# Dealing w3's rows to the partitions in neighbouring pairs, in a strided sparse attention and feed-forward kernel

## The chip, the cores and the metric

The kernel runs on one core of one Trainium2 chip. The metric is the device time of one execution in microseconds (us), and the median over several runs is compared. The engines are named as in the profile: PE is TensorE's matmul row and PEld its weight loads, DVE is VectorE, ACT is ScalarE, POOL is GpSimd, SP is SyncE. DMA transfers are issued from the queues of POOL and SP and run on 16 shared DMA engines.

## What is computed

Eight batches of 8 heads, 576 tokens and a head size of 64 go through attention. Heads 0 to 3 see a local window of 32 positions, heads 4 to 7 see every 32nd position. The result is laid out as 4,608 tokens by 512 and goes through a feed-forward part:

```python
scores = scale * np.matmul(q, k.transpose(0, 1, 3, 2))
scores = np.where(masks[None, :, :, :], scores, -1000000000.0)
scores = scores - np.max(scores, axis=-1, keepdims=True)
attn = np.exp(scores)
attn = attn / (np.sum(attn, axis=-1, keepdims=True) + 1e-09)
attn_out = np.matmul(attn, v)
...
a = x @ w1                 # 4608 x 512 by 512 x 1024
b = x @ w2
h = a * b @ w3             # 1024 x 1024
out = h @ w_out            # 1024 x 512
```

All inputs and the output are fp32; the kernel computes in fp16 with fp32 sums.

## The kernel before

**Weights.** Since nothing stands between `w3` and `w_out`, the kernel multiplies them once into `wfh` (1,024 rows by 512), and the feed-forward part becomes `(a * b) @ wfh`. All weight loads are issued from POOL and turn fp32 into fp16 on the way. `load_w3` (L210) brings two blocks of 128 rows of w3 at a time into a tile `w3s` of 128 partitions by 2 by 1,024; by the view `w3r` (L199), partition p gets rows 128 c + p and 128 (c + 1) + p, so a partition's data are two separate rows of 4 KB in memory. `load_wo` (L207) brings w_out in two halves; by the view `wor` (L200) partition p holds rows 8 p to 8 p + 7, so a half is four neighbouring rows, 8 KB in one piece. `load_w` (L203) brings w1 and w2, each in two halves of 512 columns.

**Folding.** For each of the eight blocks mc of w3's rows, `fold_t(mc)` (L218) transposes the block on PE with eight matmuls against the identity. The block is the stationary operand and is read with a step of 8 columns (L223). The result goes through PSUM into a tile `w3T` (L225). `fold_m(mc, half)` (L228) multiplies it with `woh`, four matmuls a half (L233), and after the second half the sum is copied into `wfh[:, mc, :]` (L236). Partition p of `wfh[:, mc, :]` thus belongs to the row of w3 that partition p of block mc holds.

**Feed-forward pieces.** Tokens are taken in nine chunks of 512. `emit_a(c, jc)` (L238) computes 128 columns of `x @ w1` for a chunk with four matmuls of 512 columns (L243); the weights are the stationary operand, `w1h[:, ci, jc * P:(jc + 1) * P]`. ACT copies the sum to SBUF (L247). `emit_b(c, jc)` (L250) does the same with w2 (L253), and DVE multiplies both into `abt[:, jc, :]` (L256). `emit_out` (L258) multiplies `abt` with `wfh` over all eight jc (L264), copies and stores 128 tokens. Row p of `abt[:, jc, :]` must be the same feed-forward column as partition p of `wfh[:, jc, :]`.

**Attention.** For each batch there are four pairs of heads, 32 units in all. `load_qk` (L88) and `load_v` (L108) load a unit, the q and k loads and the strided v loads from POOL, the local v loads from SP. `emit_T` transposes q and k on PE (L296), `emit_S` makes the scores (L328 local, L334 strided), `emit_max`, `emit_sub`, `emit_exp` and `emit_norm` do the softmax on DVE, ACT and POOL, `emit_P` transposes the probabilities (L396, or by DMA from unit 9 on, L391), and `emit_V` multiplies with v (L416, L433) and writes the transposed `x` into `xT`.

**Order.** Everything is issued in an order written out by hand (L498 to L714). Each engine and each DMA queue works in its own order of issue. In the start-up (L499 to L618) the first units of attention, the weight loads and the folding are interleaved: POOL issues four q and k loads of units 0 and 1, then k of unit 2, `load_w3(2, 2)`, the masks, q of unit 2, `load_w3(4, 2)`, `load_wo(0)`, unit 3, `load_wo(4)`, and later `load_w3(6, 2)` and `load_w3(0, 2)`, then w1 and w2. PE transposes units 0 and 1, makes the scores of unit 0, then comes `fold_t(2)`, the scores of unit 1, the transposes of unit 2, `fold_t(3)`, `fold_t(4)`, `fold_t(5)`, the scores of unit 2, and `fold_m(5, 0)`, the first that needs w_out. From L619 on, `feed(us, batches)` (L470) puts feed-forward pieces between the attention units: `next_piece` (L452) picks the next `emit_a`, `emit_b` or `emit_out` and counts 0.87 us for a piece of the first two kinds and twice that for the last. This order depends on counts alone, not on which columns a piece covers.

Of the kernel before, what the change touches and what calls it, by code (L numbers as in the profile page):

```python
# [9 lines left out]
FP16 = mybir.dt.float16  # L10
# [17 lines left out]
def kernel(  # L28
# [11 lines left out]
    nc = tc.nc  # L40
    B, H, S, D = q.shape
    DM = H * D
    DF = moe_w3.shape[0]
    NTOK = B * S
    P = 128
# [16 lines left out]
    wst = ctx.enter_context(tc.tile_pool(name="wst", bufs=2))  # L62
# [117 lines left out]
    w1h = wpool.tile([P, KC1, DF], FP16, name="w1h")  # L180
    w2h = wpool.tile([P, KC1, DF], FP16, name="w2h")
# [14 lines left out]

    w1r = moe_w1.rearrange("(c p) n -> p c n", p=P)
    w2r = moe_w2.rearrange("(c p) n -> p c n", p=P)
    w3r = moe_w3.rearrange("(c p) n -> p c n", p=P)  # L199
    wor = moe_w_out.rearrange("(p c) n -> p c n", p=P)  # L200
    w3st = {}

# [4 lines left out]
    def load_wo(c):  # L207
        nc.gpsimd.dma_start(woh[:, c:c + 4, :], wor[:, c:c + 4, :])

    def load_w3(c, n=1):  # L210
        w3 = wst.tile([P, n, DF], FP16, tag="w3s%d" % n, bufs=4 if n > 1 else 2, name="w3s")
        nc.gpsimd.dma_start(w3, w3r[:, c:c + n, :])
        for i in range(n):
            w3st[c + i] = w3[:, i, :]

# [12 lines left out]
    def fold_m(mc, half, eng=nc.scalar.copy):  # L228
# [6 lines left out]
        if half:  # L235
            eng(out=wfh[:, mc, :], in_=ps)  # L236

    def emit_a(c, jc):  # L238
        if jc == 0:
            abts[c] = ffn.tile([P, KC2, NT], FP16, tag="abt", name="abt")  # L240
        aps = psF.tile([P, NT], FP32, tag="f", name="aps")
        for ci in range(KC1):
            nc.tensor.matmul(aps, w1h[:, ci, jc * P:(jc + 1) * P],  # L243
                             xT[ci][:, c * NT:(c + 1) * NT], start=(ci == 0),
                             stop=(ci == KC1 - 1))
        asb = ffn.tile([P, NT], FP32, tag="asb", name="asb")
        nc.scalar.copy(out=asb, in_=aps)  # L247
        abts[c, jc] = asb

    def emit_b(c, jc):  # L250
        bps = psF.tile([P, NT], FP32, tag="f", name="bps")
        for ci in range(KC1):
            nc.tensor.matmul(bps, w2h[:, ci, jc * P:(jc + 1) * P],  # L253
                             xT[ci][:, c * NT:(c + 1) * NT], start=(ci == 0),
                             stop=(ci == KC1 - 1))
        nc.vector.tensor_mul(abts[c][:, jc, :], bps, abts.pop((c, jc)))  # L256
# [195 lines left out]
    def next_piece(batches):  # L452

        a, o = state["ab"], state["out"]
        c, j = divmod(a, 2 * KC2)
        can_ab = c < NCH and NT * c + NT <= S * batches and c < o // (NT // P) + 2
        oc, ot = divmod(o, NT // P)
        can_out = oc < NCH and a >= 2 * KC2 * (oc + 1) + (0 if c >= NCH else 2)
        late = not can_ab and oc < NCH and a >= 2 * KC2 * (oc + 1)
        if (can_out and (state["turn"] >= 4 or not can_ab)) or late:  # L460
            state["out"] += 1
            state["turn"] = 0
            return 2 * T_A, lambda: emit_out(oc, ot)
        if can_ab:
            state["ab"] += 1
            state["turn"] += 1
            return T_A, lambda: (emit_a, emit_b)[j % 2](c, j // 2)
        return None
# [29 lines left out]
    with tc.manual_schedule():  # L498
# [7 lines left out]
        load_qk(2, "k")  # L506
        emit_cast_v(1, cp)
        load_w3(2, 2)
        make_identity(nc, id16)
        make_maskL()  # L510
        zero_L(0)
        load_qk(2, "q")
        emit_T(0)
        load_w3(4, 2)
        emit_T(1)
        make_sel()
# [22 lines left out]
        emit_exp(1)  # L539
        emit_norm(0, dve)  # L540
        load_w3(6, 2)
        load_qk(4, "k")
        fold_m(4, 0)
# [202 lines left out]
```

## Time and profile before

| | |
|---|---|
| median of three runs | 269.75 us |
| the three runs | 269.6, 269.75, 272.18 us |
| the profiled execution: time | 272.12 us |
| the profiled execution: span from the first to the last instruction | 270.4 us |
| TensorE clock granted | 1.000 |
| four w3 loads, 512 KB each as fp16 | issue 794 ns in the mean, 7.5 us median from issue to landing |
| two w_out loads, 512 KB each as fp16 | issue 682 ns in the mean, 9.8 us to landing |
| 288 matmuls of w1, 288 of w2 | 74.0 and 73.9 us of PE's busy time |
| weight loads of w1 and w2 | 98 ns in the mean |

One execution was recorded by the hardware profiler. The page gives the busy time of each engine, the span in 40 equal slices of 6.8 us with a digit for the tenths in which an engine was busy, the DMA queues, the chain of work that ended last (followed back from the last instruction to whatever released each step), and the costliest groups of instructions. The trace behind it holds each instruction and each DMA packet with start and duration, so stretches of the span, the timeline of one engine and the waits of a tile can be asked for. A busy PE is not PE at its peak: matmuls overlap, so the pace is read from the distance between starts.

### The profile page before, as it was taken

The numbers are of one execution on the slowest core, as the hardware profiler recorded it, in microseconds if no ns is written. First come the engines' busy times: TensorE is split into PE (matmuls) and PEld (weight loads), VectorE is DVE, ScalarE is ACT, GpSimd is POOL, SyncE is SP. The second block draws the span as 40 slices with busy tenths as digits, with TensorE's granted clock in tenths as the row PEclk, the third lists the DMA queues.
The fourth block names the chain that finished last, engine by engine and source line by source line (L and its number), as shares of the span: only waits on it lengthen the run. The fifth ranks groups of instructions, "written<-read, shape, count | busy, mean of one in ns | idle before, by whom it ended". The sixth has DMA issues, their size and how long they took to land.

```text
span 270.4 us, 9826 instructions
## 1 busy us (share of the span) xinstructions
PE 252.0 (93%) x4186; PEld 131.5 (49%) x4186; DVE 176.2 (65%) x353; ACT 140.9 (52%) x256; POOL 153.0 (57%) x236
## 2 busy tenths in 40 slices
PE   0488999999999999899999999999999999999995
PEld 0374566445554454455555455544554444444443
DVE  2468998777788867867886788678767823332210
ACT  1561678565755654656466555545655534333322
POOL 8847767398975895489558965887674110000000
PEclk9999999999999999999999999999999999999999
DMA  7999997999999999999989998998465152001113
GB/s 118 184 199 196 190 196 113 209 164 207 221 207 156 114 229 147 172 124 211 166 129 180 221 173 77 238 189 107 85 174 102 30 93 94 2 0 71 47 55 142
DMA packets 66749, 38.75 MB, mean 143 GB/s; under 512 B 45588, under 2 KB 60944, under 8 KB 66704
## 3 DMA queue, kind: packets, MB, share of 16 engines
q0 software_dynamic: 22624, 17.29, 43.6%
q1 hardware_dynamic: 44080, 20.82, 38.2%
q8 instruction: 33, 0.54, 0.8%
q14 instruction: 12, 0.10, 0.1%
HBM read 39.24 MB, written 9.44 MB: 180 GB/s over the span
## 4 chain that ended last, share of the span: by engine, by line
PE 75%; DMA 8%; DVE 8%; POOL 4%; ACT 2%; issue 2%; SPq 0%; DVEq 0%; POOLq 0%; ACTq 0%
PE ops L264 22%; PE aps L243 19%; PE bps L253 19%; PE fps L233 4%; DMA woh<-in_moe_w_out_dram 3%; DMA pT<-prL 3%; PE op L416 2%; PE tpq L296 2%; POOL s L105 2%; PE sp L328 2%; DMA vhS<-in_v_dram 2%; DVE mx L348 1%; PE op L433 1%; PE sp L334 1%; DVE tmp L340 1%
## 5 line engine op out<-in xcount | busy, mean ns | idle before, releaser
L243 PE MATMUL aps<-xT,w1h 128*128 128x512 f16 x288 | 74.0, 379 | 0.1
L253 PE MATMUL bps<-xT,w2h 128*128 128x512 f16 x288 | 73.9, 379 | 0.0
L256 DVE TENSOR_TENSOR abt<-bps,asb 128x512 f16<-128x512 f32 x72 | 47.7, 678 | 32.7 <-PE bps L253 29.7
L264 PE MATMUL ops<-wfh,abt 128*128 128x512 f16 (+1 forms) x296 | 65.6, 374 | 0.0
L247 ACT COPY asb<-aps 128x512 f32<-128x512 f32 x72 | 41.4, 585 | 33.1 <-PE aps L243 20.1
L130 POOL DMA_DIRECT2D vhS<-in_v_dram x70 | 42.5, 717 | 5.5 <-DMA woh<-in_moe_w_out_dram 2.3
L253 PEld LDWEIGHTS <-w2h 128*128 128x128 f16 x288 | 28.2, 98 | 34.0
L264 PEld LDWEIGHTS <-abt 128*128 128x128 f16 x296 | 27.8, 98 | 30.4
L243 PEld LDWEIGHTS <-w1h 128*128 128x128 f16 x288 | 27.0, 98 | 30.7
L378 POOL TENSOR_TENSOR prS<-prS,rc 128x594 f16<-128x594 f16 x14 | 17.0, 1217 | 38.5 <-ACT asb L247 16.0
L269 ACT COPY osb<-ops 128x512 f32<-128x512 f32 (+1 forms) x36 | 20.8, 578 | 29.6 <-PE ops L264 26.7
L355 DVE TENSOR_TENSOR tmp<-tmp,mx 128x576 f32<-128x576 f32 (+1 forms) x32 | 26.1, 816 | 0.9
L105 POOL DMA_DIRECT2D s<-in_q_dram x35 | 21.0, 637 | 8.5 <-PE aps L243 3.3
L348 DVE TENSOR_REDUCE mx<-tmp 128x9 f32<-128x576 f32 (+1 forms) x32 | 24.2, 757 | 0.5
L296 PE MATMUL tpq<-id,s 54*64 54x54 f16 (+1 forms) x640 | 17.5, 196 | 7.5 <-DMA s<-in_q_dram 6.8
L105 POOL DMA_DIRECT2D s<-in_k_dram x35 | 21.4, 665 | 1.5 <-DMA s<-in_q_dram 0.9
L378 POOL TENSOR_TENSOR prL<-prL,rc 128x576 f16<-128x576 f16 x15 | 18.0, 1203 | 5.5 <-ACT osb L269 3.9
L367 ACT ACTIVATE prS<-tmp 128x594 f16<-128x594 f32 x16 | 11.2, 702 | 18.7 <-DVE tmp L355 13.1
L296 PEld LDWEIGHTS <-s 54*64 54x64 f16 (+1 forms) x1280 | 14.5, 111 | 11.5 <-DMA s<-in_q_dram 6.8
L375 DVE TENSOR_REDUCE sm<-prL 128x9 f32<-128x576 f16 x16 | 12.0, 749 | 11.3 <-ACT prL L367 11.3
L375 DVE TENSOR_REDUCE sm<-prS 128x11 f32<-128x594 f16 x16 | 12.3, 770 | 10.6 <-ACT prS L367 10.6
L296 PE MATMUL tpk<-id,s 54*64 54x54 f16 (+1 forms) x640 | 17.3, 196 | 2.0 <-DMA s<-in_k_dram 1.7
(78 smaller groups left out, 273.5 us busy)
## 6 DMA issues: line engine op xcount, KB each, us to landing
out_dram<-osb SPq DMA_DIRECT2D x35, 256.0 KB, 3.6
vsL<-in_v_dram SPq DMA_DIRECT2D x32, 128.0 KB, 5.3
s<-in_q_dram POOLq DMA_DIRECT2D x16, 144.0 KB, 4.8
s<-in_k_dram POOLq DMA_DIRECT2D x16, 144.0 KB, 4.9
s<-in_k_dram POOLq DMA_DIRECT2D x31, 74.2 KB, 4.9
s<-in_q_dram POOLq DMA_DIRECT2D x31, 74.2 KB, 4.8
w3s<-in_moe_w_dram POOLq DMA_DIRECT2D x4, 512.0 KB, 7.5
vhL<-vhL SPq DMA_DIRECT2D x16, 120.0 KB, 4.3
```

What stands on the lines that cost most here:

```text
L105: nc.gpsimd.dma_start(t[p0 + r0[0]:p0 + r0[1], h, 0:n * D], _ap(src[b, h0 + h], 0 + ap[0], ap[1] + [[1, n * D]]))
L130: nc.gpsimd.dma_start(vt[HALF * half + r0[0]:HALF * half + r0[1], h, 0:m * D], _ap(v[b, h0 + h], 6 * half * D + ap[0], ap[1] + [[1, m * D]]))
L243: nc.tensor.matmul(aps, w1h[:, ci, jc * P:(jc + 1) * P], xT[ci][:, c * NT:(c + 1) * NT], start=(ci == 0), stop=(ci == KC1 - 1))
L247: nc.scalar.copy(out=asb, in_=aps)
L253: nc.tensor.matmul(bps, w2h[:, ci, jc * P:(jc + 1) * P], xT[ci][:, c * NT:(c + 1) * NT], start=(ci == 0), stop=(ci == KC1 - 1))
L256: nc.vector.tensor_mul(abts[c][:, jc, :], bps, abts.pop((c, jc)))
L264: nc.tensor.matmul(ps, abts[c][:, jc, ts * P:(ts + 1) * P], wfh[:, jc, n * w:n * w + w], start=(jc == 0), stop=(jc == KC2 - 1))
L296: nc.tensor.transpose(tp[HALF * h:HALF * h + HALF, s, :], s16[p0:p0 + npar, h, s * D:(s + 1) * D], id16[p0:p0 + npar, p0:p0 + npar])
L348: nc.vector.tensor_reduce(out=mx, in_=tmp, axis=AX.X, op=ALU.max)
L355: nc.vector.tensor_tensor(out=tmp, in0=tmp, in1=_sub(mx, 0, P, 0, [[1, nt], [0, w]]), op=ALU.subtract)
L375: nc.vector.tensor_reduce(out=sm, in_=prv, axis=AX.X, op=ALU.add)
L378: eng.tensor_tensor(out=prv, in0=prv, in1=_sub(rc, 0, P, 0, [[1, nt], [0, w]]), op=ALU.mult)
```

## The change

The view `w3r` gives partition p the rows 256 u + 2 p and 256 u + 2 p + 1 of pair u: two neighbouring rows, 8 KB in one piece. `load_w3` copies them as one run of 2,048 columns per partition into the same tile. Block mc of w3 then holds, in partition p, row 256 (mc // 2) + 2 p + mc % 2. To match, `emit_a` and `emit_b` take for piece jc the columns 256 (jc // 2) + jc % 2 + 2 p of w1 and w2: every second column. `fold_t`, `fold_m`, `emit_out`, the order of issue and the sizes of all tiles are as before.

```diff
-    w3r = moe_w3.rearrange("(c p) n -> p c n", p=P)
+    w3r = moe_w3.rearrange("(c p i) n -> p c (i n)", p=P, i=2)
...
-    def load_w3(c, n=1):
-        w3 = wst.tile([P, n, DF], FP16, tag="w3s%d" % n, bufs=4 if n > 1 else 2, name="w3s")
-        nc.gpsimd.dma_start(w3, w3r[:, c:c + n, :])
+    def load_w3(c, n=2):
+        w3 = wst.tile([P, n, DF], FP16, tag="w3s", bufs=4, name="w3s")
+        nc.gpsimd.dma_start(w3.rearrange("p i n -> p (i n)"), w3r[:, c // 2, :])
         for i in range(n):
             w3st[c + i] = w3[:, i, :]
...
+    def cols(jc):
+        n0 = 2 * P * (jc // 2) + jc % 2
+        return slice(n0, n0 + 2 * P - 1, 2)
+
     def emit_a(c, jc):
...
-            nc.tensor.matmul(aps, w1h[:, ci, jc * P:(jc + 1) * P],
+            nc.tensor.matmul(aps, w1h[:, ci, cols(jc)],
                              xT[ci][:, c * NT:(c + 1) * NT], start=(ci == 0),
                              stop=(ci == KC1 - 1))
...
     def emit_b(c, jc):
...
-            nc.tensor.matmul(bps, w2h[:, ci, jc * P:(jc + 1) * P],
+            nc.tensor.matmul(bps, w2h[:, ci, cols(jc)],
                              xT[ci][:, c * NT:(c + 1) * NT], start=(ci == 0),
                              stop=(ci == KC1 - 1))
```

## The prediction

> **What bounds the kernel now.** I read the page's busy table and slices first, then the chain of work that ended last in order of time, then the stretches of the start-up, then the rows of the two tiles that the diff touches.
>
> ```profile
> span 270.4 us, 9826 instructions
> PE 252.0 (93%) x4186; PEld 131.5 (49%) x4186; DVE 176.2 (65%) x353; ACT 140.9 (52%) x256; POOL 153.0 (57%) x236
> ...
> PE   0488999999999999899999999999999999999995
> ...
> DMA  7999997999999999999989998998465152001113
> ```
>
> PE is full from the fifth slice nearly to the end, and the DMA engines are full from the second. So after the start-up only PE time counts: in the matmul records after 47 us the start-to-start gaps above 130 ns beyond the usual pace sum to 3.4 us, the longest 1.1 us. Before 47 us it is the chain that counts:
>
> ```profile
> 5.14 0.75 POOL w3s L212
> ...
> 8.88 0.74 POOL w3s L212
> ...
> 10.63 9.24 DMA woh<-in_moe_w_out_dram
> ...
> 19.92 5.20 PE fps L233 x16
> ...
> 47.03 0.97 PE aps L243 x4
> ```
>
> The columns are start, length, engine and tile. The first half of w_out is issued at 10.63 and lands 9.24 us later, and PE's folding starts on it. Two of the four w3 loads (issued at 5.0 and 8.8) stand ahead of it on the same queue. PE's timeline shows what else waits for them:
>
> ```profile
> 13.21 1.08 PE L223 MATMUL w3tp<-id,w3s 128*128 128x128 f16 x8 [1.08 <-DMA w3s<-in_moe_w_dram]
> ...
> 17.11 1.93 PE L223 MATMUL w3tp<-id,w3s 128*128 128x128 f16 x16 [0.49 <-DMA w3s<-in_moe_w_dram]
> ...
> 19.92 5.20 PE L233 MATMUL fps<-woh,w3T 128*128 128x512 f16 x16 [0.43 <-DMA woh<-in_moe_w_out_dram]
> ```
>
> In brackets is PE's idle time and what ended it. All three waits end with a transfer that the change speeds up or that queues behind one.
>
> **Part 1, the w3 loads.** Four loads of 512 KB go from 256 packets to 128 packets each. A packet's size in the trace is that of the fp16 written, half of the fp32 read: 2,048 B becomes 4,096 B. The new shape is already in the kernel: w_out loads four neighbouring rows of 512 columns per partition, 4,096 B written. In the packet records the median packet of w3 takes 173 ns and that of w_out 324 ns, so two old packets cost 346 ns and a new one 324: 22 ns saved, times 128 packets over 16 engines = 0.18 us a load, 0.35 us for the two ahead of w_out. By the means (199 and 193 against 358 and 327 ns) a load would save 8 x (392 - 342) = 0.4 us, 0.8 us for two. But packet times overlap on an engine, and the stretches show the pace that comes out (start and end; then busy time by engine; the last two columns are DMA share and GB/s):
>
> ```profile
> 8.50:10.00 1.50, 0.69 (x34) 0.56 (x35) 0.00 (x0) 0.75 (x3) 1.43 (x4) 1.00 1.03 185
> 12.50:14.00 1.50, 0.79 (x8) 0.80 (x8) 1.43 (x4) 0.06 (x1) 1.50 (x3) 1.00 1.09 194
> 15.00:16.50 1.50, 1.50 (x52) 1.30 (x44) 1.50 (x5) 1.15 (x3) 1.00 (x2) 1.00 1.07 209
> 24.00:26.00 2.00, 1.58 (x50) 0.72 (x47) 0.81 (x3) 0.32 (x1) 1.00 (x2) 1.00 1.14 207
> ```
>
> The first two are the early w3 loads, at about 190 GB/s; the third is mostly w_out, at 209; the fourth is the third w3 load with the short packets, at 207. So when the engines are full, short packets move as many bytes as long ones, and the gain is at most the early shortfall: 524 KB at 190 GB/s is 2.76 us, at 209 it is 2.51, so 0.25 us a load and 0.5 us for two; at least it is 0. I take the middle, 0.25 us earlier for w_out, since the early stretch is the right place but the later w3 load shows that length alone does not make the difference. The bounds are 0 and 0.5.
>
> The Trainium skill, "DMA: Bandwidth & Descriptors", section Anatomy of one DMA, prices a load as a fixed 2.0 us plus its bytes over 436 GB/s, with no term for packet length at these sizes; by it this part is worth 0, and the 207 against 209 agrees, the 190 does not.
>
> POOL's issue: a w3 issue takes 794 ns in the mean, the w_out issue in the new shape 682, so about 0.1 us less for each of four. POOL is on the chain up to 10.63, but the DMA engines are already full by then (share 1.03 to 1.09), so w_out's landing is set by the queue and I cost it at 0. If that cover were gone it would be another 0.2 us of gain. POOL's two later waits on w3s (1.3 and 1.7 us) end a little earlier; they hold up q, k and v loads that are used later, so 0.
>
> What 0.25 us earlier on w_out is worth at the end: PE's work, DVE's (which idles 1.16 us at 25.6 for PE and then 0.33 us at 31.6 for the w3 transposes) and POOL's norm at 40.9 follow from the 19.92 start, so I pass it on whole. What is late next is the second pair's transposes and the scores before 19.49, but they wait for the second w3 load, which moves too. PE's first matmuls there run at 427 ns each and at 216 from 23.2 us on; if that change of pace keeps its time, 0.25 us of slow matmuls is worth half, 0.13 us. Bounds of part 1 at the end: 0 to 0.5 us of gain, I take 0.25.
>
> **Part 2, the strided weights.** Each of the 576 weight loads of w1 and w2 now reads every second column. A matmul and its weight load are two records on two rows, and only the slower one shows:
>
> ```profile
> L223 PEld LDWEIGHTS <-w3s x64: 142/149/169, 13.2 to 37.7; 128*128 128x128 f16 x64
> ...
> L243 PEld LDWEIGHTS <-w1h x288: 95/98/99, 47.0 to 258.7; 128*128 128x128 f16 x144
> ```
>
> These are minimum, median and maximum in ns. L223 is the one load in this kernel with a step, of 8 columns: 143 ns at the fast clock against 98 packed, 45 ns more. Step 2 lies between. The 512-column matmul starts every 216 ns, and 143 is still under that, so 562 of the 576 loads stay hidden under the matmul before; the cover would be gone only above 216 ns. The other 14 follow small attention matmuls (from L296, L334 and L416), and in 13 of them the records show 111 to 125 ns from the last small matmul to the first of w1 (281 ns in the other): there the load is exposed. 14 x 45 ns = 0.63 us is the upper bound, 0 the lower, as no row gives a reason for a load with a step to be shorter than a packed one. Step 2 is nearest to the packed row, one sixth of the way in step, so I take 6 ns, 0.1 us.
>
> The Trainium skill, "SBUF — State Buffer", section Specifications (TRN2), says that reads want at least two hits per 16-byte line; every second fp16 still hits a line four times, so by it this part is 0. The 143 ns at a step of 16 bytes, one hit a line, agrees; no run here shows a step of 4 bytes.
>
> **What costs nothing.** The order of the work is the same. Pieces jc 0 to 3 still read only columns 0 to 511, so each waits for the same half of w1 and w2 as before. The transposes of w3 keep their step of 8, the fold and output matmuls their shapes; only the rows they carry are permuted.
>
> **Sum.** -0.25 + 0.1 = -0.15 us. The profiled execution took 272.12 us (span 270.4 and 1.7 around it), so it would give 272.0. It lies 2.4 us above the median of the runs, 269.75, and beside the highest, 272.18; the same change on the median gives 269.6.
>
> **Rivals.**
> *The packets change nothing* (the change does not do what it says): the 207 against 209 GB/s speaks for it, the 190 against. Then 0 + 0.1: 269.85 us. The byte price of the Trainium skill's DMA page would give this too.
> *Strided loads slow every step*: the step-8 transposes start 60 ns apart at the fast clock, the packed ones of L396 56, so 4.4 ns more per pair of load and matmul. If that is added to each pair instead of hidden, 576 x 4.4 ns = 2.5 us, and 0.6 for the exposed loads: 272.9 us, slower. At the slow clock the step-8 ones are 107 ns apart, with nothing added, which speaks for a load that is just the longer of two, and against this rival. It decides once a pair costs over 4.7 ns more (2.7 us).
> *PE's fast clock comes at another time*: 3.3 us of matmuls at 427 ns stand at 19.92, eight of them, 1.69 us more than at 216. If the earlier start meets the fast clock at once, 268.0 us; if one more such stretch follows, 271.3. The Trainium skill, "TensorE: Matmul & The Clock Gate", Part 1, says that the window that decides this runs free at 3.4 us, so both are possible; the trace's 3.3 us agrees.
> *The runs' spread*: one of three runs is 2.4 us above the other two, so a median may fall there, at 272.0.
>
> **How the numbers follow.** Forecast, between -0.5 and +0.6 us (269.2 to 270.4): 0.58. Packets nothing: 0.13. Strided loads: 0.09. Clock earlier 0.05, later 0.06. Spread: 0.09. The predicted time is 269.6 us. The range reaches from 268.8, which leaves out the clock's earlier case and a few hundredths of combinations, to 272.3, which leaves out the strided rival: about 0.15 outside. A measurement of this kernel can tell about 1% from no change, 2.7 us. Faster by more needs two gains together, 0.04; slower by more is the strided rival and the spread with a loss on top, 0.10; within 1%: 0.86.
>
> **What would show it.** Right: w3s packets of 4,096 B at 205 GB/s or more before 14 us, w_out landing before 19.9, the first w1 matmul before 47.0, L243 and L253 weight loads of 98 to 143 ns, matmul steps of 216 ns. Wrong: a w1 or w2 step above 218 ns; a first w1 matmul later than 47.2; w_out landing no earlier with faster w3 loads; a new wait on PE after 47 us.

## The result and the profile after

| | before | changed |
|---|---|---|
| median of six runs each | 270.18 us | 279.78 us |
| lowest and highest | 269.57 and 272.85 | 277.24 and 283.74 |
| profiled execution: time, span | 272.12, 270.4 | 277.24, 275.5 |

The ratio is 1.0308, with a 95% interval from 1.0262 to 1.0354; it leaves out the run of 283.74 us, which fell in a slower state. The change made the kernel 3% slower, 8.3 us by the ratio and 9.6 us between the medians, where 269.6 us and a range up to 272.3 had been forecast. The profiled execution of the changed kernel was its quickest, 5.1 us of span longer than that of before. A second profile of the changed kernel, nearer to its median, stands among the experiments.

The page of the changed kernel, its busy times and slices:

```profile
span 275.5 us, 9826 instructions
PE 253.6 (92%) x4186; PEld 131.3 (48%) x4186; DVE 175.3 (64%) x353; ACT 140.3 (51%) x256; POOL 152.3 (55%) x236
...
PE   0598995899899999999999999999999999999995
...
PEclk9999999599999999999999999999999999999999
```

The amount of work is the same. PE has a hole in the seventh slice (41 to 48 us), and in the eighth the granted clock is half. Around the hole, PE's timeline of the changed kernel (start, length, and in brackets the idle time before and what ended it):

```profile
44.30 0.39 PE L247 MATMUL aps<-xT,w1h 128*128 128x512 f16 x1
47.72 1.25 PE L247 MATMUL aps<-xT,w1h 128*128 128x512 f16 x3 [3.03 <-DMA w1h<-in_moe_w_dram]
48.77 0.63 PE L257 MATMUL bps<-xT,w2h 128*128 128x512 f16 x1
50.75 1.46 PE L257 MATMUL bps<-xT,w2h 128*128 128x512 f16 x3 [1.35 <-DMA w2h<-in_moe_w_dram]
52.00 1.91 PE L247 MATMUL aps<-xT,w1h 128*128 128x512 f16 x4
53.71 1.57 PE L257 MATMUL bps<-xT,w2h 128*128 128x512 f16 x4
```

In the kernel before, the same pieces went through without a stop:

```profile
46.96 1.04 PE L243 MATMUL aps<-xT,w1h 128*128 128x512 f16 x4
47.84 1.03 PE L253 MATMUL bps<-xT,w2h 128*128 128x512 f16 x4
```

The first feed-forward piece, jc 0, now stops after one of its four matmuls and waits for a load of w1, and the first w2 piece does the same for w2. The chain of the changed kernel names the load:

```profile
43.49 7.21 DMA w2h<-in_moe_w_dram
...
50.75 1.46 PE bps L257 x3
```

That is the load of the second half of w2, issued at 43.49 and landing 7.2 us later. Piece jc 0 reads columns 0 to 254, all in the first half. The compiled programs show why it waits all the same. These are the PE instructions of w1 and w2 that wait for a load, by their number in PE's program; in the kernel before:

```
1659 L243 Ldweights w1h [waits DMASW0_49]
1667 L253 Ldweights w2h [waits DMASW7_49]
1735 L243 Ldweights w1h [waits DMASW0_49]
1743 L253 Ldweights w2h [waits DMASW1_49]
```

and in the changed one:

```
1659 L247 Ldweights w1h [waits DMASW0_49]
1661 L247 Ldweights w1h [waits DMASW0_49]
1667 L257 Ldweights w2h [waits DMASW7_49]
1669 L257 Ldweights w2h [waits DMASW1_49]
```

`Ldweights` is a weight load; DMASW0_49 and the like are semaphores, the counters by which a DMA tells that it has landed. The first wait for DMASW0_49 in each list is for the first half of w1, the second for the second half; for w2 the halves have DMASW7_49 and DMASW1_49. The waits for the second halves have moved up from the first weight load of jc 4 to the second weight load of jc 0: from 1735 to 1661, from 1743 to 1669. The kernel does not ask for these waits. The tile framework, the software that turns the kernel into a program, puts them in where it takes two accesses of a tile to touch each other. In the tile `w1h` of 4 by 1,024 columns a half-load writes four runs of 512; those of the second half begin at 512, 1,536, 2,560 and 3,584. The slice for ci = 0 and columns 0 to 254 ends before the first of these runs begins, so the first matmul goes on. The slice for ci = 1 covers 1,024 to 1,278, between two runs of the second half, and shares no address with them. Packed, it was seen to touch none of them; with a step of 2 it is taken to touch the load whose runs lie on both sides of it. How the framework decides is not shown; the experiments test what follows from it. The compiled programs of their kernels agree: where the weights are packed (`pairs_only`), have a tile for each half, or lie in blocks (`half_major`), the second halves are first waited for at jc 4 again; in `stride_only` the wait is at the second weight load of jc 0.

The stop has a second part, the clock. In the stretches (the last three columns are granted clock, DMA share and GB/s) of the changed kernel:

```profile
45.00:50.00 5.00, 1.68 (x4) 0.37 (x4) 1.07 (x4) 1.78 (x4) 0.00 (x0) 0.80 1.23 209
50.00:55.00 5.00, 4.25 (x11) 1.58 (x12) 2.27 (x4) 0.58 (x1) 0.16 (x1) 0.52 0.33 75
```

After the first idle time the granted clock falls: it is 0.52 in the mean of the second stretch, and in the trace's clock records it is 0.5 from 48.0 to 54.8 us. Matmuls in it start up to 427 ns apart instead of 216.

### The profile page after: what moved, and what is told of

It reads as the page before. It is cut to its first block, busy times and chain, and to the rows that moved or that the text cites. A ratio compares the mean times of both kernels' runs of the same rounds, so it can differ in the third digit from the quotient of the medians.

```text
span 275.5 us, 9826 instructions
## 1 busy us (share of the span) xinstructions
PE 253.6 (92%) x4186; PEld 131.3 (48%) x4186; DVE 175.3 (64%) x353; ACT 140.3 (51%) x256; POOL 152.3 (55%) x236
## 4 chain that ended last, share of the span: by engine, by line
PE 72%; DMA 8%; DVE 8%; POOL 4%; ACT 3%; issue 2%; SPq 1%; DVEq 0%; POOLq 0%; ACTq 0%
PE ops L268 21%; PE bps L257 20%; PE aps L247 19%; DMA w2h<-in_moe_w_dram 3%; PE fps L233 3%; DMA w3s<-in_moe_w_dram 3%; PE tpq L300 2%; PE op L420 2%; DMA vsL<-in_v_dram 2%; POOL s L105 2%; DMA vhS<-in_v_dram 2%; PE sp L332 1%; DVE tmp L359 1%; PE sp L338 1%; DVE sm L379 1%
## 5 line engine op out<-in xcount | busy, mean ns | idle before, releaser
L247 PE MATMUL aps<-xT,w1h 128*128 128x512 f16 x288 | 75.6, 385 | 3.0 <-DMA w1h<-in_moe_w_dram 3.0
L257 PE MATMUL bps<-xT,w2h 128*128 128x512 f16 x288 | 75.5, 385 | 1.4 <-DMA w2h<-in_moe_w_dram 1.4
L251 ACT COPY asb<-aps 128x512 f32<-128x512 f32 x72 | 41.2, 584 | 40.1 <-PE aps L247 27.0
L359 DVE TENSOR_TENSOR tmp<-tmp,mx 128x576 f32<-128x576 f32 (+1 forms) x32 | 25.2, 786 | 0.9
```

The source lines that it names most:

```text
L247: nc.tensor.matmul(aps, w1h[:, ci, cols(jc)], xT[ci][:, c * NT:(c + 1) * NT], start=(ci == 0), stop=(ci == KC1 - 1))
L257: nc.tensor.matmul(bps, w2h[:, ci, cols(jc)], xT[ci][:, c * NT:(c + 1) * NT], start=(ci == 0), stop=(ci == KC1 - 1))
L359: nc.vector.tensor_tensor(out=tmp, in0=tmp, in1=_sub(mx, 0, P, 0, [[1, nt], [0, w]]), op=ALU.subtract)
```

## The experiments

Theory A is the false wait, a wait for a load that the piece does not read. Theory B is the rival of the prediction: the step in the weight loads costs time by itself. Theory C: the quicker w3 loads bring PE to the feed-forward part before its weights have landed.

**Each half of the change alone, and the change with the false wait taken away.** Four kernels, with 29 runs of the kernel before beside them (median 270.88 us).

`pairs_only`, w3 in pairs, packed columns:

```diff
-            nc.tensor.matmul(aps, w1h[:, ci, cols(jc)],
+            nc.tensor.matmul(aps, w1h[:, ci, jc * P:(jc + 1) * P],
```

and the same in `emit_b`.

> w3 is loaded in neighbouring pairs, but the pieces of w1 and w2 take packed columns as before, so rows of the folded weights and columns of the pieces are not matched and the output differs; the amount and order of work are those of before. Theory A (the strided column slice makes the second matmul of the very first w1 piece and of the first w2 piece wait for the second half-loads of w1 and w2): no such wait here, feed-forward starts near 44.3 us as in the changed kernel instead of 47.0 and goes on without a stop, so 266.5 to 269.5 us against 270. Theory B (the weight loads with a step are themselves slow, or lower the clock): the same, 266.5 to 270. Theory C (the earlier start of the folding, from the w3 loads, runs PE into weights that have not landed): PE waits for w1 and w2 here too, 274 to 280 us.

Measured: 271.03 us, ratio 1.0012 (0.9982 to 1.0043). PE waits for neither w1 nor w2, so theory C falls. There is no gain either: the first piece starts at 47.0 us and not near 44.3, and the time is above the upper end of what A and B expected.

`stride_only`, w3 as before, columns with a step:

```diff
-    w3r = moe_w3.rearrange("(c p i) n -> p c (i n)", p=P, i=2)
+    w3r = moe_w3.rearrange("(c p) n -> p c n", p=P)
...
-        nc.gpsimd.dma_start(w3.rearrange("p i n -> p (i n)"), w3r[:, c // 2, :])
+        nc.gpsimd.dma_start(w3, w3r[:, c:c + n, :])
```

> w3 is loaded as before, the pieces of w1 and w2 take every second column; rows and columns are not matched, so the output differs, with the same amount and order of work. Theory A: the first w1 piece waits near 47 us for the second half of w1, which landed at about 50.1 us in the kernel before, and the first w2 piece for that of w2 at about 53.9: 5 to 6 us of idle time on PE and some microseconds at the slow clock, 276 to 281 us. Theory B: 272.5 to 279 us with no longer wait at the first piece, but slower steps throughout. Theory C: 269.5 to 271 us.

Measured: 279.39 us, ratio 1.0295 (1.0246 to 1.0344), the loss of the whole change. This agrees with A and not with C, and by its time alone it agrees with B to within 0.4 us. PE's timeline shows the waits of A, 3.0 us for w1 and 1.9 us for w2.

`pairs_stride_two_tiles`, the whole change with a tile for each half:

```diff
-    w1h = wpool.tile([P, KC1, DF], FP16, name="w1h")
+    w1h = [wpool.tile([P, KC1, DF // 2], FP16, name=f"w1h{i}") for i in range(2)]
...
-        nc.gpsimd.dma_start(dst[:, :, n], src[:, :, n])
+        nc.gpsimd.dma_start(dst[half], src[:, :, n])
...
-            nc.tensor.matmul(aps, w1h[:, ci, cols(jc)],
+            nc.tensor.matmul(aps, w1h[jc // 4][:, ci, cols(jc)],
```

with `cols` counted inside the half, and the same for w2.

> The whole change, with w1 and w2 held in one tile for each half of the columns, so that a strided slice can only touch the half that it reads. Theory A: the early waits for the second halves are gone, PE starts feed-forward near 44.3 us and goes on: 266.5 to 269.5 us, faster than before by 0.3 to 1.3%. Theory B: still 276 to 281 us, as the weight loads keep their step. Theory C: 274 to 280 us, with PE waiting at the first pieces for the first halves or soon after for the second.

Measured: 271.03 us, ratio 0.9994 (0.9963 to 1.0024). The step is still there, the loss is not. Its PE timeline:

```profile
47.43 1.04 PE L247 MATMUL aps<-xT,w1h 128*128 128x512 f16 x4
48.30 1.03 PE L257 MATMUL bps<-xT,w2h 128*128 128x512 f16 x4
```

Four matmuls in one go, at the old pace. Theory B falls. The gain that A expected beside it did not come.

`stride_two_tiles`, the same without the pairs, to price the step by itself:

> w3 is loaded as before, the pieces take every second column, and each half of w1 and w2 has its own tile; rows and columns are not matched, so the output differs, with the same amount and order of work. This prices the step of the weight loads by itself. Theory A: 269.5 to 271 us, at most 0.6 us above before from 14 exposed weight loads. Theory B: 272.5 to 279 us. Theory C: 269.5 to 271 us.

Measured: 270.74 us, ratio 1.0001 (0.9967 to 1.0036). The step costs nothing that can be measured.

**The wait alone, without any step.** `second_half_first` is the kernel before, in which the first token chunk starts with pieces jc 4 to 7:

```diff
-            return T_A, lambda: (emit_a, emit_b)[j % 2](c, j // 2)
+            jc = (j // 2 + 4) % KC2 if c == 0 else j // 2
+            return T_A, lambda: (emit_a, emit_b)[j % 2](c, jc)
```

> The kernel before, packed columns and w3 as before, but the first token chunk takes its pieces in the order jc 4 to 7, then 0 to 3, so that its first piece truly needs the second halves of w1 and w2. No step in any weight load. If the wait for the second halves is the whole loss (theory A), this kernel loses as the changed one does: PE idles some 2.5 to 3 us at the first w1 piece and 1.5 to 4 us at the first w2 piece, then a stretch of slow matmuls, 276 to 281 us. If the strided reads have a part in it (theory B), 270 to 274 us.

Measured: 281.23 us, ratio 1.0349 (1.0268 to 1.0431), 0.2 us above what A expected. PE's timeline shows the same picture:

```profile
50.16 1.89 PE L243 MATMUL aps<-xT,w1h 128*128 128x512 f16 x4 [3.25 <-DMA w1h<-in_moe_w_dram]
54.17 1.89 PE L253 MATMUL bps<-xT,w2h 128*128 128x512 f16 x4 [2.12 <-DMA w2h<-in_moe_w_dram]
```

So a wait for the second halves at this place is enough for the whole loss, with packed weights and the old w3 loads.

**The weights in one tile, but with each half as a block.** `half_major`:

```diff
-    w1h = wpool.tile([P, KC1, DF], FP16, name="w1h")
+    w1h = wpool.tile([P, 2, KC1, DF // 2], FP16, name="w1h")
...
-            nc.tensor.matmul(aps, w1h[:, ci, cols(jc)],
+            nc.tensor.matmul(aps, w1h[:, jc // 4, ci, cols(jc)],
```

> The whole change, each weight in one tile as before, but with the half of the columns as the outermost index (2 by 4 by 512 instead of 4 by 1,024 per partition), so that a half is one unbroken block. If what counts is that the address range spanned by a strided slice runs across the other half's load, the early waits go with this alone: 269.5 to 271.5 us, as with two tiles. If any strided slice of a tile is taken to touch every load into that tile, the waits stay: 277 to 281 us. By theory B (the step itself is slow) also 277 to 281.

Measured: 271.48 us beside 271.74, ratio 1.0002 (0.9953 to 1.0051). A step within one tile is no trouble where the other half's load is one unbroken block beside the slice, and not runs on both sides of it.

**The second halves earlier.** `after_early_halves` is the changed kernel with the two second half-loads issued behind the norm of unit 3 instead of behind those of units 4 and 5:

```diff
         emit_norm(3)
+        load_w(w1r, w1h, 1)
+        load_w(w2r, w2h, 1)
         shift_v(0)
```

> The changed kernel with the second half-loads of w1 and w2 issued from POOL right behind the norm of unit 3, ahead of the norms of units 4 and 5; by the trace they go out 1.7 and 2.8 us earlier. Theory A: the waits at the first pieces shrink by about that much, the w2 one decides, and a shorter stop keeps more of the clock: 274 to 277.5 us. Theory B: no change, 278.5 to 281 us. If POOL's later norms are what PE needs next, part of the gain is lost, up to 1.6 us.

Measured: 275.64 us, ratio 1.0184 (1.0087 to 1.028). By the ratios about 3 of the 8 us come back. Who PE waits for from 40 to 66 us (in total, times, longest):

```profile
PE bps L257 <- DMA w2h<-in_moe_w_dram: 1.6, 1, 1.6
PE op L420 <- issue: 1.6, 1, 1.6
```

The wait for w1 is under the list's threshold, and the matmuls after the stop run at 216 ns. `after_earliest` issues both still earlier, directly behind the first half of w2.

> The changed kernel with the second half-loads of w1 and w2 issued directly behind the first half of w2, ahead of the norms of units 3, 4 and 5; the weights have then landed before or about when the first piece starts. Theory A: the wait at the first pieces is gone or under 1 us, 270 to 274 us, less than the 275.6 of the smaller move; what is left is what the loads take from the transfers and norms that they are now ahead of. Theory B: 278 to 281 us.

Measured: 274.12 us, ratio 1.0099 (1.0055 to 1.0142), a little above the range that A gave, and by the medians better than the smaller move, though the two intervals overlap. The wait did not go, as A had expected: in the profiled execution (275.94 us, the second longest of ten) PE still stood 1.2 us for w1 and 1.5 us for w2. The second half of w2 was issued at 40.4 us instead of 45.4 in `after_again` (the changed kernel's second profile, below), but it landed only at 50.9 instead of 52.4. So the loss that is left still holds some of the wait; what else is in it was not separated. Over the profiled executions with such waits the time goes roughly with that landing: 49.6 us (`after_early_halves`, 273.75), 50.7 (the changed kernel's first profile, 277.24), 50.9 (`after_earliest`, 275.94), 51.9 (`after_filler`, below, 279.29), 52.4 (`after_again`, 280.03) and 54.1 (`second_half_first`, 282.08).

**The changed kernel once more.**

> The changed kernel once more, for a profile beside the first, whose 277.24 us is the lowest of its runs. Theory A: the first piece again stops at its second matmul until the second half of w1 lands and the first w2 piece until that of w2; the first w1 matmul comes between 44 and 47.5 us, and the end is 277 to 283 us, later the later the start-up was.

Measured: 280.03 us, one execution, span 278.2. Its first piece starts at the same 46.96 us as in the kernel before, so the two can be set side by side. PE:

```profile
46.97 0.39 PE L247 MATMUL aps<-xT,w1h 128*128 128x512 f16 x1
48.91 0.82 PE L247 MATMUL aps<-xT,w1h 128*128 128x512 f16 x3 [1.55 <-DMA w1h<-in_moe_w_dram]
49.57 0.38 PE L257 MATMUL bps<-xT,w2h 128*128 128x512 f16 x1
52.42 0.99 PE L257 MATMUL bps<-xT,w2h 128*128 128x512 f16 x3 [2.47 <-DMA w2h<-in_moe_w_dram]
53.21 1.91 PE L247 MATMUL aps<-xT,w1h 128*128 128x512 f16 x4
54.91 1.74 PE L257 MATMUL bps<-xT,w2h 128*128 128x512 f16 x4
...
60.28 1.03 PE L247 MATMUL aps<-xT,w1h 128*128 128x512 f16 x4
```

By the matmul records the first two w1 matmuls start 1.95 us apart instead of 0.22, the first two of w2 2.85 instead of 0.22: 4.4 us of standing still. Two pieces take 1.70 and 1.58 us from start to start instead of 0.86: 1.6 us of slow clock. Together that is about 6, and piece jc 4 starts at 60.3 instead of 54.2, 6.1 us late. There is a second stop, from what was queued behind the first. DVE and ACT of this kernel:

```profile
53.52 0.69 DVE L260 TENSOR_TENSOR abt<-bps,asb 128x512 f16<-128x512 f32 x1 [5.25 <-PE bps L257]
```

```profile
73.05 0.72 ACT L280 CAST vhL<-vsL 128x640 f16<-128x640 f32 x1 [3.87 <-DMA vsL<-in_v_dram]
73.68 0.63 ACT L308 COPY kTL<-tpk 128x576 f16<-128x576 f16 x1
```

```profile
74.36 0.49 PE L400 MATMUL pp<-id,prS 128*128 128x128 f16 x6 [1.01 <-ACT kTL L308]
```

DVE stands 5.25 us at its first product, and behind it in DVE's order stand the maximum of unit 7 and the sums of unit 6. POOL's norm waits for those sums 9.9 us, where it waited 5.1 before, and behind the norm POOL issues the next q, k and v loads, 4.0 us later than before. SP's next loads of v stand behind copies that wait for ACT; they go out at 65.1 us instead of 59.1, and ACT waits 3.9 us for them (1.7 before). PE then stops again at 73 us: its next matmul starts 1.4 us after the last instead of 0.2. The order of these records fits one chain; no run takes it apart. The first piece of the second token chunk starts 7.6 us late (79.9 against 72.3), and the span ends 7.8 us late.

**Without the slow clock.** `after_filler` puts matmuls with no use on PE while it would stand idle:

```diff
+        filler(12)
         feed(0.65, 1)
+        filler(6)
         feed(1.67, 1)
```

where `filler(n)` runs n matmuls of 128 by 512 columns of w_out into a PSUM tile that nobody reads.

> The changed kernel with 12 matmuls of 512 columns on w_out, whose result is not used, put on PE ahead of the first w1 piece, and 6 ahead of the first w2 piece; they keep PE at work while it would wait for the second halves. This splits the loss: theory A1 (idle time and the slow clock after it share it, about 5 and 2.5 us): the slow matmuls after the wait go, 276 to 278 us against about 279.8 for the changed kernel. Theory A2 (it is idle time alone, the slow clock is hidden by other work): no change, 279 to 281 us. If the fillers were longer than the wait they would add up to 1 us.

Measured: 279.8 us, ratio 1.0299 (1.0219 to 1.038), no gain. By its time this is A2, but its PE timeline shows something else:

```profile
46.55 2.76 PE L494 MATMUL wps<-woh 128*128 128x512 f16 x12
49.15 1.03 PE L247 MATMUL aps<-xT,w1h 128*128 128x512 f16 x4
50.01 1.46 PE L494 MATMUL wps<-woh 128*128 128x512 f16 x6
51.30 0.38 PE L257 MATMUL bps<-xT,w2h 128*128 128x512 f16 x1
51.91 0.82 PE L257 MATMUL bps<-xT,w2h 128*128 128x512 f16 x3 [0.23 <-DMA w2h<-in_moe_w_dram]
52.57 1.03 PE L247 MATMUL aps<-xT,w1h 128*128 128x512 f16 x4
...
70.71 5.30 PE L268 MATMUL ops<-wfh,abt 128*128 128x512 f16 x16 [3.12 <-issue]
```

The clock stayed up and piece jc 4 started at 58.1, two microseconds sooner than in `after_again`; then PE stopped for 3.1 us at 67.4, longer than the second stop of the changed kernel, and slow matmuls followed there. That stop is marked "issue", so the profile shows nothing that it waits for. A block of 16 KB on the DMA queue for instructions ended at 69.35 us, 1.4 us before PE went on; the gaps near 45 us, told of below, look the same. So the time that the fillers won may have gone into a wait for instructions, which was not tested. What the slow clock alone is worth at the end stays open.

## Why the prediction was wrong

**The step that failed** is in the part "What costs nothing": "Pieces jc 0 to 3 still read only columns 0 to 511, so each waits for the same half of w1 and w2 as before." The first half of the sentence holds, the second does not follow. What a piece reads and what it is made to wait for are two things. With a step, a slice that lies between the runs of the second half's load is made to wait for that load, though it shares no address with it. The prediction put this term at nothing. In its place `after_again`, beside an equal start of the first piece, shows 4.4 us of standing still at two waits (1.55 and 2.47 us idle in PE's rows), 1.6 us of matmuls at the slow clock and 1.2 us of a second stop, about 7 of the 7.8 us by which its span is longer. None of the rivals named it. The one with the right sign, strided loads that slow every step, has the wrong mechanism: `pairs_stride_two_tiles` and `stride_two_tiles` keep every step and lose nothing.

**Part 1, the w3 loads**: right in that it is worth little; whether it is 0.25 us or nothing the runs do not resolve. The second w3 load landed at 16.0 to 17.1 us in the eight profiled executions with pairs and at 16.4 to 18.0 in the three with separate rows whose landing is on record, 0.7 us sooner in the mean. The packets of the first half of w_out behind it, counted in the order of their starts, ended at 18.4 to 19.0 us in the four with separate rows and at 18.4 to 19.3 in the eight with pairs: 18.7 in the mean in both. That speaks for the 207 against 209 GB/s of the prediction, and for its lower bound, 0. The folding began at 19.2 to 20.8 us with separate rows and at 18.8 to 19.9 with pairs, and in seven of the twelve the wait before it ended with DVE's copy of `w3T`, not with w_out. So w_out's landing is not alone in setting this start, as the prediction had it. At the end `pairs_only` lies between 0.5 us faster and 1.2 us slower than before, which holds 0 and 0.25 alike.

**The prediction passed a gain of the start-up on whole; these profiles do not.** In `pairs_only` the folding began at 19.3 us instead of 19.9, but the first w1 piece at 47.0 as before. Between them, PE's timeline of `pairs_only`:

```profile
45.39 0.30 PE L420 MATMUL op<-pT,vhL 64*64 64x32 f16 x16 [1.20 <-issue]
```

The kernel before has 0.33 us there and goes on at 45.34. A block of 16 KB on the instruction queue ended at 44.03 us in `pairs_only` and at 44.08 before, and PE went on 1.3 us later in both; in the first profile of the changed kernel the block was in at 40.1 and there was no such gap. A gap at this place, of 0.3 to 1.6 us, stands in seven of the twelve profiles, and in each the block ended 1.3 to 1.6 us before PE went on. That PE waits there for its own instructions fits these records; it was not tested. Nor does the gap belong to the pairs: in `stride_two_tiles`, with separate rows, the folding began at 19.2 us, there was no such gap, and the first piece started at 46.5.

**Part 2, the step of the weight loads**: 0.1 us was taken between 0 and 0.63 (a step of 2 is one seventh, not one sixth, of the way from 1 to 8; both give 0.1); in the weight loads' own times it is 0. The weight loads of w1 in `half_major`:

```profile
L247 PEld LDWEIGHTS <-w1h x288: 96/98/102, 46.2 to 258.6; 128*128 128x128 f16 x144
```

98 ns, as packed. By the Trainium skill, "SBUF — State Buffer", section Specifications (TRN2), two hits per 16-byte line are enough, and a step of 4 bytes has four; the 98 ns agrees.

**The clock's time** did move. In the first profile of the changed kernel the folding ran at 216 ns from the start:

```profile
18.82 3.61 PE L233 MATMUL fps<-woh,w3T 128*128 128x512 f16 x16 [0.39 <-DMA woh<-in_moe_w_out_dram]
```

Sixteen matmuls take 3.61 us instead of 5.20, and the first piece starts at 44.3 instead of 47.0; 1.1 of these 2.7 us were there when the folding began. It is the rival "fast clock at another time", and with the false wait its gain went into a longer wait. `stride_only`, with the old w3 loads, had it too (first piece at 44.6), so it is not the doing of the pairs.

No version that was run beats the kernel before: `pairs_stride_two_tiles` and `half_major` equal it.

## What to carry to other kernels

When an edit turns a packed slice of a tile into a strided one, look in the compiled program at which instruction each load is first waited for: a wait can come in though not one more byte is read. Where a tile is filled by several loads, lay it out so that each load writes one unbroken block (or give each its own tile). And a quicker load ahead in the queue need not bring the load behind it sooner: here, with the DMA engines full and the bytes the same, the packets of w_out ended at 18.7 us with either form of the w3 loads.

## What the runs showed of the hardware that was not expected

Two short idle times were followed by the half clock: 1.55 and 2.47 us with 1.0 us of matmuls between them in `after_again` (half clock from 52.9 to 56.3 us, matmuls 427 ns apart, 1.6 us lost), and 1.2 and 1.5 us in `after_earliest` (from 50.6 to 54.0). In `after_early_halves` an idle time of 1.6 us for w2 was not. Weight loads of 128 by 128 fp16 took 98 ns at steps of 2 and 4 bytes alike and 143 to 148 at 16, at the fast clock. And PE stood 0.3 to 1.6 us near 45 us in seven of the twelve profiles, going on 1.3 to 1.6 us after a block on the instruction queue had ended; whether the one causes the other is not shown.
